# A fused attention and mixture-of-experts kernel: recurrent products in all four quadrants, counts by two blocks, eight tie blocks on GpSimd, other PSUM banks

## The chip, the cores and the metric

The kernel runs on one core of a Trainium2 chip. The metric is the device time of one execution in microseconds (us). The core has five engines with queues of their own: TensorE (PE in the profile, its weight loads PEld), VectorE (DVE), ScalarE (ACT), GpSimd (POOL) and SyncE (SP, which issues most DMAs). Each engine works its queue in order; semaphores tie them together.

## The reference

Three stages follow one another. The first is linear attention with a decaying state, over two batches, eight heads, 768 positions and head size 64:

```python
intra = (q_b @ k_b.T * Dmask) @ v_b                  # within a block
inter = (q_b * lam_pow) @ kv_state                   # from the blocks before
out[block] = intra + inter
kv_state = lam_block * kv_state + (k_b * rev_pow).T @ v_b
```

Its output, as 1536 tokens of 512 numbers, goes through a dense layer, `g = h * clip(h + 3, 0, 6) / 6` with `h = x @ w_in` (512 to 2048), then `x2 = g @ w_out` (2048 to 512). The third stage sends each token to one of eight experts: all pairs of token and expert are walked through from the highest logit down, a pair is taken if the token is still free and the expert has fewer than 192 tokens, and each token then goes through its expert, `relu(x2 @ w1[e]) @ w2[e]` (512 to 1024 to 512).

## The kernel before

Attention (`attention`, L425) works in twelve chunks of 128 positions, six a batch (`s = c % 6`). The head size is 64, so two heads of a pair share the 128 partitions; a chunk has four head pairs `hp` with two halves `par`. PE makes the scores `S` (L451), DVE masks them into `sm` (L457), PE multiplies the decayed keys `kd` with the values into `kv` (L466). The state lives in three SBUF tiles `sbd`: DVE fades the old one into the new (L471) and adds `kv` (L473); the first chunk of a batch only copies (L475). Then `outs` puts the chunk's output `xo` together in one PSUM bank, head pair by head pair: a product of the state with the decayed queries `qd` for each half (L489, if there is a state, which holds for ten of the twelve chunks) and one of `sm` with the values (L492). All are float32. Of a state product the operands of half 0 lie in partitions 0 to 63 and its output goes to 0 to 63, half 1 has 64 to 127 for both. ACT (L496) and DVE (L497) turn `xo` into two float16 halves of `xT`, which the dense layer takes.

Every product of the dense layer is three float16 products (`mm3`, L221 to L223, tile `h`). Its weights come as 64-bit integers, and `weights` decodes them on ACT, DVE (tiles `wid`, `wod`) and POOL. ACT and DVE make `g` from `h` (`r`, L526 and L527). The second layer is `x2_part` (L637, tile `x2p`): 48 matmuls for each of twelve token blocks, 512 columns wide for the first eight blocks, 384 for the last four, whose remaining 128 columns are made last (192 matmuls). Its output goes to `xa` and `xb`.

The routing runs beside x2: its logits come from `g` and a projected gate, and it takes seven phases. In each, PE spreads every token's current value over the partitions (`mp`, L738), ACT copies it to SBUF (`mrow`), and for each of twelve token blocks a mask `G` says which tokens come before which: below (L770) and at or below (L779) on DVE, four blocks on ACT for the first part. Tokens of equal value inside a block are ordered by a tie block `eq`: `BY_GE = 6` on POOL (L746, one selection over all at L748), the others on DVE (L753). PE counts with four matmuls a block (`count`, L792, tile `cp`) and twelve small ones for the ties (`ties`, L763). Then DVE compares with the capacity (`F`), PE spreads the result (`sm`, L809 and L810), and DVE settles the next phase. After the last phase come the ranks (`rk`) and positions (`pos`), POOL scatters the rows of `xa` and `xb` to DRAM (L840), they come back by expert (`xs`), and the experts run (`hp`, L885, `po`, L915).

The order of each engine's queue is written by a planner (`Plan`) when the kernel is built. It keeps a clock for each engine, and places the step that can begin first by its own costs, among those within a small window the one with the lowest key. A step with no free PSUM or SBUF slot in its pool waits. PSUM has eight banks in pools: pA 3, pB 2, pC 2, pE 1. Routing steps have the key `GK = -1e6` and go first; x2's matmuls fill PE's time between them, one at a time.

Of the kernel before, what the change touches and what calls it, by code (L numbers as in the profile page):

```python
# [5 lines left out]
F32 = mybir.dt.float32  # L6
# [9 lines left out]
P = 128  # L16
# [176 lines left out]
def fused_kernel(ctx, tc, raw_d, lam_d, win_d, wout_d, wg_d, w1_d, w2_d, out):  # L193
# [227 lines left out]
    out_done = {}  # L421
# [3 lines left out]
    def attention(c, key):  # L425
# [33 lines left out]
        if s < 5:  # L459
            pk = buf("pC", [P, 4, 64], F32, f"kv{c}")  # L460

            def kv():
                for hp in range(4):
                    for par in range(2):
                        cl = slice(P * hp + 64 * par, P * hp + 64 * par + 64)
                        te.matmul(pk[64 * par:64 * par + 64, hp], kd[:, cl], r[:, 2, cl], start=True, stop=True)  # L466
            t_kv = add("pe", 0.66, kv, [t_kd] + ld, [kd, r, pk], key)
# [26 lines left out]
        used = [r, po] + sms + ([qd, sbdb] if s else [])  # L494
        t_o = out_done[c] = add("pe", 3.9 if s else 1.95, outs, t_mk + t_qd + ld + (state_done[c - 1] if s else []), used, key)
        t_h = add("se", 0.48, lambda: se.activation(x[:, 0, :, t0:t0 + P], po[:], AF.Copy, scale=2.0 ** 10), [t_o], [po, x], key)  # L496
        x_done[c] = add("ve", c_ve(512), lambda: ve.scalar_tensor_tensor(  # L497
            x[:, 1, :, t0:t0 + P], po[:], 2.0 ** 10, x[:, 0, :, t0:t0 + P], op0=OP.mult, op1=OP.subtract), [t_h], [po, x], key)
# [6 lines left out]
    def h_unit(g, u, key, lo_eng):  # L505
# [17 lines left out]
        t = add("pe", 12 * nf * c_pe(T), mms, w_done[f0 % 4 // 2:(f0 % 4 + nf - 1) // 2 + 1] + [x_done[c] for c in cs], [w, x, ps], key)  # L523
# [42 lines left out]
    def project(k, t, dst):  # L566
# [11 lines left out]
        t_pj.append(add("pe", 0.5, pj, tr + [t_wg], [wt, wpp], key))  # L578
# [112 lines left out]
    BY_GE = 6  # L691
# [38 lines left out]
    for p in range(PHASES):  # L730
# [12 lines left out]
        eqs = [buf("Q", [P, 6, P], BF, f"eq{p}_{i}") for i in range(2)]  # L743
# [4 lines left out]
        t_eq = [add("ge", 1.3, lambda eq=eqs[0]: ge.affine_select(  # L748
# [10 lines left out]
        def ties(cp=cp, eqs=eqs):  # L759
            for f in range(3):  # L760
                for k in range(4):
                    b = 3 * k + f
                    te.matmul(cp[32 * k:32 * k + 32, P * f:P * f + P], ohc[:, b], eqs[b // BY_GE][:, b % BY_GE], start=False, stop=False)  # L763
        order_c = [0, 1, 2, 11, 3, 4, 10, 5, 9, 6, 8, 7]
        for n, i in enumerate(order_c):
# [24 lines left out]
            def count(i=i, n=n, G=G, z=z, cp=cp):  # L790
                for k in range(4):
                    te.matmul(cp[32 * k:32 * k + 32, :], ohc[:, i], G[:, z, 384 * k:384 * k + 384], start=(n == 0),  # L792
                              stop=(n == NCH - 1))
# [170 lines left out]
def pack(inputs):  # L964
# [12 lines left out]
    lam = np.repeat(np.asarray(inputs["lam"]).reshape(4, 2).T, 64, axis=0)  # L977
# [22 lines left out]
```

## Time and profile before

| | us |
|---|---|
| median of 3 runs | 525.7 (525.66 to 525.78) |
| the profiled execution | 526.52 |
| its span in the trace | 524.5 |
| PE busy | 498.5 (95%) |
| DVE busy | 404.6 (77%) |
| ACT busy | 300.6 (57%) |
| POOL busy | 156.0 (30%) |

The mean granted clock of PE is 0.983 of full speed. Busy shares are means over stages that differ: the dense layer with attention runs to about 205 us, the routing beside x2 to about 346, then come the ranks, the scatter and the rest of x2, and from 391 on the experts. A wait in a row of PE stands in brackets behind it, with the engine that ended it; "issue" means that nothing in the profile explains it.

### The profile page before, as it was taken

The page shows a single profiled execution, that of the slowest core. Times are in us where ns is not written, and L with a number is a line of the kernel's source. Part 1 is how long each engine was busy: PE and PEld are TensorE (multiplying, and loading weights), DVE is VectorE, ACT ScalarE, POOL GpSimd, SP SyncE. Part 2 cuts the span into 40 slices and gives each one's busy share as a digit, 9 for nine tenths or more (in the row PEclk, how much of TensorE's full clock was granted, in tenths as well). Part 3 has the DMA queues.
Part 4 walks back from the last instruction along what each step waited for, and adds up shares of the span by engine and source line. Part 5 has one row for each costly group of instructions (what it writes and reads, how often), then busy time and mean ns, then how long its engine had stood idle before and what let it go on. Part 6 is the DMA issues. An engine that isn't in the chain of part 4 may idle for free.

```text
span 524.5 us, 10556 instructions
## 1 busy us (share of the span) xinstructions
PE 498.5 (95%) x4378; PEld 304.5 (58%) x4378; DVE 404.6 (77%) x718; ACT 300.6 (57%) x444; POOL 156.0 (30%) x160
## 2 busy tenths in 40 slices
PE   7898999998999999999999999999499999999995
PEld 3566454687786444534433443466399577786762
DVE  7799999999534988699899888975242988889620
ACT  1547958563235574287669667843152867778610
POOL 2022424040000340055325523628811122223111
PEclk8999999999999999999999999999779999999999
DMA  7999524202537224000000001746454999998011
GB/s 217 396 417 413 196 87 164 81 2 53 142 129 161 41 41 81 2 1 1 1 2 1 1 0 56 267 176 212 118 144 125 358 332 417 290 377 349 4 41 40
DMA packets 44912, 77.88 MB, mean 148 GB/s; under 512 B 33081, under 2 KB 34113, under 8 KB 38721
## 3 DMA queue, kind: packets, MB, share of 16 engines
q1 hardware_dynamic: 42752, 70.82, 41.0%
q0 software_dynamic: 2112, 6.39, 3.3%
q8 instruction: 34, 0.56, 0.5%
q14 instruction: 14, 0.11, 0.1%
HBM read 63.46 MB, written 6.40 MB: 133 GB/s over the span
## 4 chain that ended last, share of the span: by engine, by line
PE 61%; DVE 21%; issue 9%; DMA 5%; ACT 2%; POOL 1%; POOLq 0%; SPq 0%; DVEq 0%; ACTq 0%
PE x2p L637 24%; PE hp L885 8%; PE po L915 6%; PE h L221 4%; PE h L222 4%; PE h L223 4%; PE cp L792 3%; DMA ws<-w 2%; DVE r L527 2%; DVE g L415 2%; DVE wid L388 2%; DVE wid L390 2%; PE mp L738 1%; DMA raw<-raw 1%; ACT kd L438 1%
## 5 line engine op out<-in xcount | busy, mean ns | idle before, releaser
L637 PE MATMUL x2p<-wo,g 128*128 128x512 f16 (+2 forms) x768 | 144.7, 334 | 7.5 <-issue 7.1
L637 PEld LDWEIGHTS <-g 128*128 128x128 f16 x768 | 65.4, 102 | 63.7 <-issue 22.5
L221 PE MATMUL h<-xT,wi 128*128 128x256 f16 (+2 forms) x304 | 88.3, 301 | 3.7 <-DVE r L527 3.7
L223 PE MATMUL h<-xT,wi 128*128 128x256 f16 (+2 forms) x304 | 88.2, 300 | 0.0
L222 PE MATMUL h<-xT,wi 128*128 128x256 f16 (+2 forms) x304 | 88.2, 300 | 0.0
L415 DVE SCALAR_TENSOR_TENSOR w<-ws,w 128x1024 f16<-128x1024 f32 x58 | 71.5, 1277 | 8.1 <-ACT w L405 7.3
L746 POOL TENSOR_SCALAR eq<-mrow,m 128x128 bf16<-128x128 f32 x42 | 47.3, 1142 | 85.4 <-DVE on L719 60.2
L405 ACT ACTIVATE w<-ws 128x1024 f16<-128x1024 f32 x64 | 64.3, 1049 | 2.9 <-DMA ws<-w 2.2
L885 PE MATMUL hp<-xs,w 128*128 128x192 f16 x768 | 65.1, 246 | 0.0
L885 PEld LDWEIGHTS <-w 128*128 128x128 f16 x768 | 63.1, 98 | 3.2 <-issue 1.6
L915 PE MATMUL po<-w,h 128*64 128x512 f16 (+1 forms) x384 | 64.1, 380 | 0.1
L384 POOL TENSOR_SCALAR wod<-wod 128x1024 f32<-128x1024 f32 x8 | 23.7, 2965 | 103.5 <-ACT wod L382 103.5
L526 ACT ACTIVATE r<-h,c 128x512 f32<-128x512 f32 (+1 forms) x52 | 33.3, 646 | 30.6 <-PE h L223 30.6
L779 DVE TENSOR_SCALAR G<-mrow,m 128x1408 bf16<-128x1408 f32 (+10 forms) x77 | 48.2, 648 | 0.0
L915 PEld LDWEIGHTS <-h 128*64 128x64 f16 (+1 forms) x384 | 29.0, 104 | 31.7 <-issue 1.6
L405 ACT ACTIVATE g<-r 128x512 f16<-128x512 f32 (+1 forms) x52 | 30.2, 592 | 23.0 <-DVE r L527 19.8
L415 DVE SCALAR_TENSOR_TENSOR g<-r,g 128x512 f16<-128x512 f32 (+1 forms) x52 | 35.7, 697 | 9.2 <-ACT g L405 8.8
L527 DVE SCALAR_TENSOR_TENSOR r<-r,h 128x512 f32<-128x512 f32 (+1 forms) x52 | 32.9, 640 | 11.4 <-ACT r L526 11.3
L222 PEld LDWEIGHTS <-wi 128*128 128x128 f16 x304 | 29.7, 98 | 17.3 <-issue 4.2
L773 ACT ACTIVATE G<-mrow,m 128x1536 bf16<-128x1536 f32 (+3 forms) x28 | 39.3, 1404 | 0.2
L221 PEld LDWEIGHTS <-wi 128*128 128x128 f16 x304 | 29.7, 98 | 14.8 <-issue 0.7
L223 PEld LDWEIGHTS <-wi 128*128 128x128 f16 x304 | 29.7, 98 | 14.6
(147 smaller groups left out, 685.1 us busy)
## 6 DMA issues: line engine op xcount, KB each, us to landing
ws<-w SPq DMA_DIRECT2D x32, 1024.0 KB, 9.3
raw<-raw SPq DMA_DIRECT2D x24, 512.0 KB, 9.8
wis<-w_in SPq DMA_DIRECT2D x8, 1024.0 KB, 14.9
wos<-w_out SPq DMA_DIRECT2D x8, 1024.0 KB, 6.3
tab<-tz SPq DMA_DIRECT2D x1, 512.0 KB
wt<-wo SPq DMA_TRANSPOSE x16, 3.4
xsa<-xa,pos POOLq DMA_INDIRECT x12
xsb<-xb,pos POOLq DMA_INDIRECT x12
```

The costliest lines, as they stand in the source:

```text
L221: te.matmul(ps, lh, rh, start=start, stop=False)
L222: te.matmul(ps, lh, rl, start=False, stop=False)
L223: te.matmul(ps, ll, rh, start=False, stop=stop)
L405: h = add("se", c_se(n), lambda: se.activation(dst()[0], src(), AF.Copy, scale=sc), deps, bufs, key, reserve)
L415: lo = add("ve", c_ve(n), lambda: ve.scalar_tensor_tensor(dst()[1], src(), sc, dst()[0], op0=OP.mult, op1=OP.subtract), [h], bufs, key)
L527: t = add("ve", c_ve(nf * T), lambda: ve.scalar_tensor_tensor(r[:], r[:], 6.0 * 2.0 ** -11, ps[:], op0=OP.min, op1=OP.mult), [t], [ps, r], ...
L637: te.matmul(ps[:], gsl(y, fc, j), w[:, z, fc % 4, d0:d1], start=(fc + y + z == 0), stop=(fc == 15 and y == 1))
L746: t_eq.append(add("ge", 1.06, lambda i=i, eq=eqs[0], mrow=mrow: ge.tensor_scalar(eq[:, i], mrow[:, P * i:P * i + P], m[:, i:i + 1], None, ...
L773: se.activation(G[:, z, 0:o], mrow[:, 0:o], AF.Sign, scale=-1.0, bias=m[:, i:i + 1])
L779: ve.tensor_scalar(G[:, z, o:], mrow[:, o:], m[:, i:i + 1], None, op0=OP.is_le)
L885: te.matmul(ps[:, i], w[:, z, kk % 2, cl], x[:, 2 * kk + y, CAP * i0:CAP * i0 + CAP], start=(i + kk + y + z == 0), stop=(i == 1 and kk == ...
L915: te.matmul(o, h1[e][:, y, k, cl], w2[e, fh][0][:, zz, f], start=(k + y + zz == 0), stop=(k == 7 and y == 1))
```

## The change

1. The host swaps the two partition halves of every odd head pair in q, k and lam. With that, a state product of an odd pair reads partitions 0 to 63 and writes 64 to 127, or the reverse. `outs` goes by halves `h2` of two head pairs: four state products, then four intra-chunk ones; even and odd pairs have a PSUM bank each (both of pC). ACT and DVE take `xT` from the two banks with two instructions each in place of one.
2. The fade of the state is done by ACT, in four instructions of 64 columns, and `kdec` is filled by four copies.
3. `kv` of the chunks from 4 on is in pool pE; the projection of the gate waits for `kv` of chunk 10.
4. `x2p` of each third token block is in pool pB.
5. A `count` step takes two blocks, and the ties come ahead of the last pair.
6. `BY_GE` is 8: POOL makes eight tie blocks and one selection over 1024 columns, DVE four, with a key ahead of the masks.

```diff
-            pk = buf("pC", [P, 4, 64], F32, f"kv{c}")
+            pk = buf("pE" if c > 3 else "pC", [P, 4, 64], F32, f"kv{c}")
...
-                        cl = slice(P * hp + 64 * par, P * hp + 64 * par + 64)
+                        cl = slice(P * hp + 64 * (par ^ hp & 1), P * hp + 64 * (par ^ hp & 1) + 64)
...
-                t = state_read[c] = add("ve", 0.35, lambda: ve.tensor_tensor(
-                    sb, old, pw[:, :, 256:257].to_broadcast([P, 4, 64]), op=OP.mult), war + state_done.get(c - 1, []), [tabb, sbdb], key)
+                def fade():
+                    for hp in range(4):
+                        se.activation(sb[:, hp], old[:, hp], AF.Copy, scale=pw[:, hp, 256:257])
+                t = state_read[c] = add("se", 0.8, fade, war + state_done.get(c - 1, []), [tabb, sbdb], key)
...
-        po = buf("pC", [P, 4, P], F32, f"xo{c}")
+        pos = [buf("pC", [P, 2, P], F32, f"xo{c}_{z}") for z in range(2)]
...
-            for hp in range(4):
-                for par in range(2):
-                    pr = slice(64 * par, 64 * par + 64)
-                    if s:
-                        te.matmul(po[pr, hp], sp[pr, hp], qd[pr, hp], start=True, stop=False)
-                for par in range(2):
-                    h = 2 * hp + par
-                    te.matmul(po[64 * par:64 * par + 64, hp], r[:, 2, 64 * h:64 * h + 64], sms[par][:, hp],
-                              start=(s == 0), stop=True)
+            for h2 in range(2):
+                if s:
+                    for z in range(2):
+                        for par in range(2):
+                            pr, o = slice(64 * par, 64 * par + 64), 64 * (par ^ z)
+                            te.matmul(pos[z][o:o + 64, h2], sp[pr, 2 * h2 + z], qd[pr, 2 * h2 + z], start=(h2 == 0), stop=False)
+                for z in range(2):
+                    for par in range(2):
+                        h = 2 * (2 * h2 + z) + par
+                        te.matmul(pos[z][64 * par:64 * par + 64, h2], r[:, 2, 64 * h:64 * h + 64], sms[par ^ z][:, 2 * h2 + z],
+                                  start=(s == 0 and h2 == 0), stop=(h2 == 1))
...
-        if j < JB:
-            x2_part(j, 0, 512, "pC", x_key + 11 * j)
-        else:
-            x2_part(j, 0, 384, "pC", x_key + 11 * j)
+        x2_part(j, 0, 512 if j < JB else 384, "pB" if j % 3 == 2 else "pC", x_key + 11 * j)
...
-    BY_GE = 6
+    BY_GE = 8
...
-                t_eq.append(add("ve", 0.27, lambda i=i, tie=tie: tie(i), [t_row[i // 4]], [eqs[1], mrow], GK + n))
+                t_eq.append(add("ve", 0.27, lambda i=i, tie=tie: tie(i), [t_row[i // 4], t_oh], [eqs[1], mrow], GK - 0.5))
...
+            group.append((i, z, G))
+            t_g += t
+            if len(group) < 2:
+                continue
```

The planner writes the queues anew from this. On PE, the first state chunk's output `xo` (chunk 1) began like this before; `qd` and `sbd` are the state product's operands, `sm_0` and `sm_1` the masked scores of the two halves:

```order
L489 MATMUL xo_317<-qd_238,sbd 64x128 x2
L492 MATMUL xo_317<-sm_0_248,raw_110 64x128
L492 MATMUL xo_317<-sm_1_278,raw_110 64x128
L489 MATMUL xo_317<-qd_238,sbd 64x128 x2
L492 MATMUL xo_317<-sm_0_248,raw_110 64x128
L492 MATMUL xo_317<-sm_1_278,raw_110 64x128
```

The same chunk on PE now (`xo_0` and `xo_1` are the two banks):

```order
L494 MATMUL xo_0_385<-qd_238,sbd 64x128 x2
L494 MATMUL xo_1_386<-qd_238,sbd 64x128 x2
L498 MATMUL xo_0_385<-sm_0_259,raw_110 64x128
L498 MATMUL xo_0_385<-sm_1_281,raw_110 64x128
L498 MATMUL xo_1_386<-sm_1_281,raw_110 64x128
L498 MATMUL xo_1_386<-sm_0_259,raw_110 64x128
```

Both pieces are half a chunk: four state products and four intra-chunk ones, in four turns before and in two now. On DVE, the second routing phase began like this before:

```order
L723 SCALAR_TENSOR_TENSOR ohc<-closed,oh 128x12x8
L770 TENSOR_SCALAR G_0_2842<-mrow_2827,m 128x128
L770 TENSOR_SCALAR G_0_2842<-mrow_2827,m 128x256
L779 TENSOR_SCALAR G_0_2842<-mrow_2827,m 128x1408
L779 TENSOR_SCALAR G_0_2842<-mrow_2827,m 128x1280
L770 TENSOR_SCALAR G_1_2866<-mrow_2827,m 128x384
L779 TENSOR_SCALAR G_1_2866<-mrow_2827,m 128x1152
L753 SCALAR_TENSOR_TENSOR eq_1_2878<-mrow_2827,m,before 128x128
L770 TENSOR_SCALAR G_1_2866<-mrow_2827,m 128x512
L779 TENSOR_SCALAR G_1_2866<-mrow_2827,m 128x1024
```

The same phase on DVE now:

```order
L729 SCALAR_TENSOR_TENSOR ohc<-closed,oh 128x12x8
L777 TENSOR_SCALAR G_0_2904<-mrow_2890,m 128x128
L777 TENSOR_SCALAR G_0_2904<-mrow_2890,m 128x256
L759 SCALAR_TENSOR_TENSOR eq_4_2911<-mrow_2890,m,before 128x128 x4
L786 TENSOR_SCALAR G_0_2904<-mrow_2890,m 128x1408
L786 TENSOR_SCALAR G_0_2904<-mrow_2890,m 128x1280
L777 TENSOR_SCALAR G_1_2936<-mrow_2890,m 128x384
L786 TENSOR_SCALAR G_1_2936<-mrow_2890,m 128x1152
L777 TENSOR_SCALAR G_1_2936<-mrow_2890,m 128x512
L786 TENSOR_SCALAR G_1_2936<-mrow_2890,m 128x1024
```

DVE's four tie blocks of a phase stand together ahead of the second half of the first masks; before, six were spread over the phase. On PE a phase from the second on held 10 matmuls of x2 before its first count and 57 in all, with nine interruptions by counts; now 19 stand before the first count and 38 before the ties, 58 in all, with six interruptions. The instructions after the ranks stand in the same order on every engine as before.

## Rows read from the trace of the kernel before

**Rows 1.** Stretches: start:end, length, busy PE, PEld, DVE, ACT, POOL, clock, DMA, GB/s

```profile
20.00:122.00 102.00, 95.62 (x960) 64.22 (x960) 99.77 (x141) 67.57 (x145) 28.20 (x9) 1.00 0.54 205
122.00:205.00 83.00, 81.59 (x694) 50.16 (x692) 60.55 (x84) 41.12 (x61) 11.41 (x4) 1.00 0.40 94
205.00:346.00 141.00, 140.71 (x1137) 62.46 (x1136) 124.06 (x320) 96.18 (x103) 55.63 (x52) 1.00 0.11 38
370.00:382.00 12.00, 4.89 (x35) 2.91 (x35) 2.44 (x3) 0.98 (x2) 8.27 (x14) 0.63 0.51 138
391.00:519.00 128.00, 127.44 (x1157) 92.17 (x1154) 86.47 (x112) 75.79 (x101) 29.39 (x32) 1.00 0.70 237
```

**Rows 2.** Waits of PE from 20 to 135 us: total, times, longest

```profile
PE h L221 <- DVE r L527: 3.7, 4, 1.3
```

**Rows 3.** Timeline of PE: start, length, line, tile, count [idle before <-releaser]; chunk 8

```profile
124.27 0.43 PE L489 MATMUL xo<-qd,sbd 64*64 64x128 f32 x4 [1.37 <-DVE sbd L473]
...
127.21 1.16 PE L451 MATMUL S<-raw 64*128 64x128 f32 x16
```

**Rows 4.** Timeline of PE: the first chunk, which has no state

```profile
16.22 1.09 PE L492 MATMUL xo<-sm,raw 128*64 128x128 f32 x16 [1.46 <-DMA raw<-raw]
17.12 1.46 PE L466 MATMUL kv<-raw,kd 128*64 128x64 f32 x16
```

**Rows 5.** Lines: duration ns min/median/max, first and last start us

```profile
L471 DVE TENSOR_TENSOR sbd<-sbd,tab x8: 415/424/861, 21.2 to 129.7; 128x256 f32<-128x256 f32 x8
L497 DVE SCALAR_TENSOR_TENSOR xT<-xo,xT x12: 682/684/692, 20.6 to 148.8; 128x512 f16<-128x512 f32 x12
L438 ACT ACTIVATE kd<-raw,kdec x80: 331/333/348, 16.2 to 98.9; 128x64 f32<-128x64 f32 x80
```

**Rows 6.** Timeline of PE in one phase of the routing (the second)

```profile
238.74 1.47 PE L738 MATMUL mp<-ident,m 128*128 128x128 f32 x12
240.05 2.32 PE L637 MATMUL x2p<-wo,g 128*128 128x512 f16 x10
242.30 0.35 PE L792 MATMUL cp<-G,ohc 128*32 128x384 bf16 x4
242.58 0.82 PE L637 MATMUL x2p<-wo,g 128*128 128x512 f16 x3
243.33 0.35 PE L792 MATMUL cp<-G,ohc 128*32 128x384 bf16 x4
...
244.58 0.51 PE L792 MATMUL cp<-G,ohc 128*32 128x384 bf16 x8
...
253.20 0.34 PE L763 MATMUL cp<-eq,ohc 128*32 128x128 bf16 x12
...
255.03 1.89 PE L637 MATMUL x2p<-wo,g 128*128 128x512 f16 x8
256.75 0.93 PE L738 MATMUL mp<-ident,m 128*128 128x128 f32 x7
```

**Rows 7.** Timeline of POOL in the same phase, and its tie line in all phases

```profile
240.07 6.78 POOL L746 TENSOR_SCALAR eq<-mrow,m 128x128 bf16<-128x128 f32 x6 [9.32 <-DVE on L719]
246.92 0.97 POOL L748 TENSOR_SCALAR_AFFINE_SELECT eq<-eq 128x768 bf16<-128x768 bf16 x1
...
L746 POOL TENSOR_SCALAR eq<-mrow,m x42: 622/1213/1812, 221.9 to 335.5; 128x128 bf16<-128x128 f32 x42
```

**Rows 8.** Timeline of DVE in the same phase: two masks of 512 columns

```profile
244.26 0.47 DVE L770 TENSOR_SCALAR G<-mrow,m 128x512 bf16<-128x512 f32 x1
...
251.85 0.47 DVE L779 TENSOR_SCALAR G<-mrow,m 128x512 bf16<-128x512 f32 x1
```

**Rows 9.** Timeline of PE from the end of x2 to the experts

```profile
370.43 0.22 PE L637 MATMUL x2p<-wo,g 128*128 128x128 f16 x1 [0.45 <-issue]
...
381.15 1.12 PE L637 MATMUL x2p<-wo,g 128*128 128x128 f16 x9 [0.43 <-issue]
...
391.11 2.06 PE L885 MATMUL hp<-xs,w 128*128 128x192 f16 x23
```

More of the change, by code (lines that the diff above doesn't have):

```diff
@@ L494, in attention @@
[L494 to L498, printed above, removed]
+            for h2 in range(2):
[4 more added lines that the diff above has]
+                            te.matmul(pos[z][o:o + 64, h2], sp[pr, 2 * h2 + z], qd[pr, 2 * h2 + z], start=(h2 == 0), stop=False)
+                for z in range(2):
+                    for par in range(2):
+                        h = 2 * (2 * h2 + z) + par
+                        te.matmul(pos[z][64 * par:64 * par + 64, h2], r[:, 2, 64 * h:64 * h + 64], sms[par ^ z][:, 2 * h2 + z],
+                                  start=(s == 0 and h2 == 0), stop=(h2 == 1))
@@ new lines, in attention @@
+        used = [r] + pos + sms + ([qd, sbdb] if s else [])
+        t_o = out_done[c] = add("pe", 3.0 if s else 1.6, outs, t_mk + t_qd + ld + (state_done[c - 1] if s else []), used, key)
+        done = []
+        for z in range(2):
+            t_h = add("se", 0.31, lambda z=z: se.activation(x[:, 0, z::2, t0:t0 + P], pos[z][:], AF.Copy, scale=2.0 ** 10), [t_o], [pos[z], x], key)
+            done.append(add("ve", 0.34, lambda z=z: ve.scalar_tensor_tensor(
+                x[:, 1, z::2, t0:t0 + P], pos[z][:], 2.0 ** 10, x[:, 0, z::2, t0:t0 + P], op0=OP.mult, op1=OP.subtract), [t_h], [pos[z], x], key))
@@ L501, in fused_kernel @@
+        x_done[c] = done
     gb, g_done = {}, {}
@@ L742, in fused_kernel @@
         t_oh = add("ve", 2.0 if p else 1.4, (lambda: (choose(), open_only())) if p else pick0, [t_m], [], GK)
-        eqs = [buf("Q", [P, 6, P], BF, f"eq{p}_{i}") for i in range(2)]
+        eqs = [buf("Q", [P, n, P], BF, f"eq{p}_{n}") for n in (BY_GE, NCH - BY_GE)]
         t_eq = []
@@ L762, in ties @@
                     b = 3 * k + f
-                    te.matmul(cp[32 * k:32 * k + 32, P * f:P * f + P], ohc[:, b], eqs[b // BY_GE][:, b % BY_GE], start=False, stop=False)
+                    te.matmul(cp[32 * k:32 * k + 32, P * f:P * f + P], ohc[:, b], eqs[b >= BY_GE][:, b % BY_GE], start=False, stop=False)
         order_c = [0, 1, 2, 11, 3, 4, 10, 5, 9, 6, 8, 7]
+        group, t_g = [], []
         for n, i in enumerate(order_c):
@@ L787, in fused_kernel, with count @@
             if i >= BY_GE:
-                t_eq.append(add("ve", 0.27, lambda i=i, tie=tie: tie(i), [t_row[i // 4]], [eqs[1], mrow], GK + n))
[L790 to L793, printed above, removed]
+                t_eq.append(add("ve", 0.27, lambda i=i, tie=tie: tie(i), [t_row[i // 4], t_oh], [eqs[1], mrow], GK - 0.5))
[3 more added lines that the diff above has]
+                continue
+            def count(group=group, n=n, cp=cp):
+                for i, z, G in group:
+                    for k in range(4):
+                        te.matmul(cp[32 * k:32 * k + 32, :], ohc[:, i], G[:, z, 384 * k:384 * k + 384], start=(n == 1 and i == group[0][0]),
+                                  stop=(n == NCH - 1 and i == group[1][0]))
             if n == NCH - 1:
-                t_c = add("pe", 0.4, ties, [t_c, *t_eq], eqs + [cp], GK)
-            t_c = add("pe", 0.24, count, t + [t_c, t_oh], [G, cp], GK)
+                t_c = add("pe", 0.2, ties, [t_c, *t_eq], eqs + [cp], GK)
+            t_c = add("pe", 0.44, count, t_g + [t_c, t_oh], [x[2] for x in group] + [cp], GK)
+            group, t_g = [], []
         t = t_c
@@ L976, in pack @@
     raw = np.stack([x.reshape(nb * c, P, 512) for x in parts], axis=2)
-    lam = np.repeat(np.asarray(inputs["lam"]).reshape(4, 2).T, 64, axis=0)
+    for x in (raw[:, :, 0], raw[:, :, 1]):
+        x = x.reshape(nb * c, 2, 64, 4, P)
+        x[:, :, :, 1::2] = x[:, ::-1, :, 1::2].copy()
+    lam = np.asarray(inputs["lam"]).reshape(4, 2).T.copy()
+    lam[:, 1::2] = lam[::-1, 1::2].copy()
+    lam = np.repeat(lam, 64, axis=0)
     wi = np.asarray(inputs["moe_w_in"]).reshape(4, P, 8, 256).transpose(2, 1, 0, 3)
```

14 lines of the change are left out of this document (7 added, 7 removed).

## The prediction

> **What bounds the kernel now.** On the page TensorE (PE) has by far the largest busy share, so a change gains about what it takes out of PE's queue, wherever PE is not waiting for something else. The table of stretches says where that is [rows 1]. From 20 to 122 us VectorE (DVE) is busy for 99.77 of 102 us and PE for 95.62: here DVE decodes weights and is the limit, and PE's waits say so (3.7 us in four waits of the first GEMM for DVE's product `r`, up to 1.3 us each) [rows 2]. From 122 to 205 us PE is busy for 81.59 of 83, from 205 to 346 (the routing) for 140.71 of 141, from 391 to 519 (the experts) for 127.44 of 128. In between lies one hole: from 370 to 382 us PE works for 4.89 of 12 us. There the last 128-column matmuls of x2 come in bursts, with waits that the profile calls "issue", until the row at 381.15; the experts start at 391.11 [rows 9]. The expert part has no slack, so whatever moves its start moves the end by as much.
>
> **The change, part by part.**
>
> *Recurrent products.* In the chunk at 124.27 PE goes from the first product to the next tile at 127.21 in 2.94 us [rows 3]: eight groups, by turns 64\*64 and 128\*64 in tiling, at 2.94/8 = 0.367 us. A chunk without state runs all its sixteen 128\*64 passes in one mode, two side by side, from 16.22 to 17.12: eight steps in 0.90 us, 0.11 each [rows 4]. In the new order a chunk has four groups: two 64\*64 groups that now use all four quadrants, and two 128\*64 groups with twice the passes. I price the first as before, 0.367, since four products side by side are as deep as two; the second is 0.367 + 2 x 0.11 = 0.587. A chunk takes 2 x (0.367 + 0.587) = 1.91 us and saves 1.03. Ten chunks have a state. No row of before shows four quadrants at once; if they run two after two, the 64\*64 group is 0.587 deep as well, the chunk takes 2.35 and saves 0.59.
>
> Five of these chunks lie where PE is at most waiting for itself (one at 96.5 us, four from 124.27 on): 5 x 1.03 = 5.2 us on the path. The other five lie in DVE's stretch, where PE's time is hidden behind DVE. There DVE decides: six of the eight state fades go (0.42 us each [rows 5]: -2.5 us), and eight evacuations of xT are cut in two. A whole one is 0.684 us for 512 columns; the fade's 0.424 for 256 gives 0.26 for 256 columns and so about 0.16 of fixed cost, which each cut adds once (+1.3 us). DVE has 1.2 us less to do, which I take as the gain of this stretch, 1.3 us; nothing of it is the lower bound, and the upper is 3.5, about PE's waits for DVE there [rows 2]. ScalarE's four small fades take 4 x 0.333 = 1.3 us at most (the copy of kd has their size [rows 5]), DVE's one took 0.42; the chain fade, sum, next chunk becomes up to 0.9 us longer. At 124.27 PE already waited 1.37 us for that chain [rows 3]. The new order puts the kv products earlier, in a bank of their own, which should take that wait away, and the longer chain may keep it: I count nothing, with 0 to 1.4 in the range. Sum for attention: 5.2 + 1.3 = **6.5 us**, between 4 (five chunks at 0.59, and 1 early) and 9 (5.2 + 3.5).
>
> *Counts by two blocks.* One phase of the routing takes 256.75 - 238.74 = 18.0 us, and there are seven [rows 6]. PE fills a phase with 57 matmuls of x2; eight of them take 1.72 us (255.03 to 256.75), 0.215 each. A single count costs 242.58 - 242.30 = 0.28 us, and a run of three x2 matmuls between two counts takes 243.33 - 242.58 = 0.75 us, 0.10 more than 3 x 0.215. A double count is 0.51 instead of 0.35 long, so 0.16 more than a single [rows 6]. Merging two singles saves 0.28 + 0.10 - 0.16 = 0.22 us. Nine interruptions become six: 0.66 us a phase. With 58 instead of 57 matmuls of x2 in the phase, it is 18.0 - 0.66 + 0.22, about 17.6 us: the ranks come 7 x 0.41 = 2.9 us earlier, and x2 as a whole is done 7 x 0.66 = 4.6 less about 0.2 = 4.4 us earlier.
>
> *Eight tie blocks on GpSimd.* GpSimd starts 1.33 us after the phase's first product, takes 6.78 us for six blocks and 0.97 for the selection: it ends at 247.89, 9.2 us into the phase, and PE uses the ties at 253.20, 14.5 us in [rows 6, 7]. Two blocks more at 1.13 and a selection of 0.97 x 8/6 = 1.29 (an estimate) end at 11.8 us. PE now reaches the ties after 38 matmuls of x2: 1.31 (from the first product to the first x2 matmul, 238.74 to 240.05) + 38 x 0.215 + 5 x 0.44 + 5 x 0.10 = 12.2 us in. The margin is 0.4 us, so GpSimd costs nothing, but the cover is nearly gone: each 0.1 us on every block puts 0.8 us on the phase once the margin is used. On DVE two tie blocks go (2 x 0.27) and four move ahead of the second half of the first pair of counts, which come 4 x 0.27 = 1.1 us later; 19 matmuls of x2 stand before the first count now, against 10, which is 1.9 us of cover. The later pairs on DVE are level with PE to some 0.3 us; I leave 0 to 0.4 us a phase (0 to 3 in all) as a loss, and take 0.
>
> By the Trainium skill, page "SBUF — State Buffer", section "Who interferes with whom", VectorE and GpSimd share a port as an exclusive lock, so that one waits wholly for the other. By that two more blocks of 0.62 us (GpSimd's shortest) could stop DVE for 1.24 us a phase where it gets back 0.54, some 5 us in seven phases. The rows speak against it for this form: DVE's 128x512 comparison takes 0.47 us at 244.26, with GpSimd at work, and 0.47 at 251.85, with GpSimd done [rows 8]; it is GpSimd whose blocks spread from 0.622 to 1.812 [rows 7].
>
> *x2 in a third bank, kv in its own.* A third bank frees PE from DVE's evacuation; PE hardly waits for it in the routing (0.3 of 141 us), so it is worth nothing, to +0.3. The projections now wait for the tenth chunk's kv product; the products they sat behind come first anyway: nothing.
>
> *The hole at 370 us.* The order after the ranks is the same on every engine. The bursts end about when the gathered rows of the experts arrive, and GpSimd's scatters run through them (8.27 of 12 us [rows 1]). If the hole hangs on the scatters, it moves with the ranks and the experts start 6.5 + 2.9 = 9.4 us earlier; if it has a fixed length, with x2, 6.5 + 4.4 = 10.9. From the side of the unpriced losses (0 to 3 us in DVE's pairs, half of it) 1 us comes off. I take **9 us**.
>
> The profiled execution took 526.52 us, 2.0 more than its span of 524.5 and 0.8 more than the median of 525.7. 526.52 - 9 = 517.5 in its own terms, which is 525.7 - 9 = **516.7 us** as a median.
>
> **The rivals.**
>
> *Quadrants in pairs.* If four products don't run side by side, ten chunks save 0.59: five late ones give 3.0, and the rest as above, 1.3 + 2.9 - 1 = 6.2 to 7 us in all: 519. For it: no row of before has more than two. Against it: two on the diagonal do run together.
>
> *DVE takes it.* The early stretch gives nothing and PE meets new waits for DVE's pairs in the routing at the upper bound: 5.2 + 2.9 - 3, about 4 to 5 us: 521.5. For it: 99.77 of 102 us; against it: DVE's own list gets shorter in both places.
>
> *The hole shrinks.* No wait in the profile explains it. If the shift of 1.5 us between ranks and x2 takes the tail out of it, up to 10 us go on top: 507. Against it: the same order on all engines.
>
> *Slower: GpSimd late.* PE waits for eight blocks in each phase. With a mean block of e, GpSimd ends at 1.33 + 8e + 1.29, against 12.2: no wait to e = 1.2, and 8 x (e - 1.2) us a phase above it. Nine us over seven phases are 1.28 a phase, so from e = 1.36 on the kernel is slower than before; at 1.45 it is 14 us, some 530. For it: the median of 1.213 and single blocks up to 1.812 [rows 7], which six in a row averaged out to 1.13; against it: those six took the same 6.7 to 6.8 us in each phase.
>
> **How the numbers follow.** The forecast (all four parts as priced) 0.6, quadrants in pairs 0.12, DVE takes it 0.12, the hole shrinks 0.08, GpSimd late 0.08 (of which 0.05 ends slower and 0.03 within a few us of before). Range: the forecast's own bounds are 4 + 2.9 - 1 = 6 and 9 + 4.4 = 13.4 us of gain, 512 to 520; taking in the DVE case it reaches to 522.5, and the quadrant case lies within: 511.5 to 522.5 leaves out the hole, GpSimd and little else. A difference under about 0.2% (1 us) can't be told from none in this kernel's runs. Faster by more 0.9, within 0.05, slower 0.05.
>
> **What would show it.** Right: a chunk's products of about 1.9 us with four quadrant rows at one start; phases of about 17.6 us; GpSimd's selection ending before the tie products; the ranks some 9 us and the experts' first row some 9 to 11 us earlier (near 382). Wrong: chunks of 2.3 us; PE waits named after `eq` or `G` in the routing; a hole of another length than 11 us ahead of the experts.

## The result, and the profile of the changed kernel

The changed kernel took 519.88 us (median of 4 runs, 518.49 to 520.86) against 525.74 us before (4 runs, 525.66 to 526.39): 0.9884 of the time, 95% interval 0.9859 to 0.9909. That is 5.9 us less, where 9 were forecast (516.7 us); it lies inside the range and on the forecast side. The profiled execution is the quickest of the four, 518.49 us with a span of 516.7, so its span is 7.8 us shorter than before. Run again on two other chips (e8 and e12, below), the changed kernel took 8.9 and 7.6 us less than the kernel before.

The page's first part for the changed kernel, busy time by engine, and two of its groups (instructions of a line, busy us, mean ns of one):

```profile
PE 485.8 (94%) x4381; PEld 301.6 (58%) x4383; DVE 398.9 (77%) x710; ACT 309.3 (60%) x488; POOL 163.5 (32%) x174
...
L752 POOL TENSOR_SCALAR eq<-mrow,m 128x128 bf16<-128x128 f32 x56 | 56.7, 1030 | 84.5 <-DVE on L725 52.1
...
L786 DVE TENSOR_SCALAR G<-mrow,m 128x1408 bf16<-128x1408 f32 (+10 forms) x77 | 52.0, 706 | 0.0
```

The stretches of the changed kernel (columns as in [rows 1]; the fourth is its hole, which now lies from 361 to 373 us):

```profile
20.00:122.00 102.00, 95.99 (x1036) 67.65 (x1034) 97.45 (x146) 74.21 (x181) 24.36 (x8) 0.98 0.53 202
122.00:205.00 83.00, 82.16 (x762) 49.91 (x763) 64.08 (x96) 45.19 (x72) 13.83 (x5) 1.00 0.39 96
205.00:346.00 141.00, 138.51 (x1079) 64.31 (x1069) 122.93 (x307) 96.07 (x101) 69.70 (x69) 1.00 0.13 47
361.00:373.00 12.00, 3.50 (x18) 1.41 (x18) 2.97 (x3) 2.38 (x3) 7.80 (x16) 0.61 0.47 120
384.00:512.00 128.00, 126.64 (x1146) 91.36 (x1143) 85.40 (x111) 75.33 (x100) 29.50 (x33) 1.00 0.69 237
```

From 20 to 122 us DVE is no longer full (97.45 of 102 us). From 205 on PE is idle for 2.5 us where it was idle for 0.3 before. The waits of PE in that stretch name the cause (total us, times, longest); before there was no wait for `G` in this list:

```profile
PE cp L805 <- DVE G L786: 2.5, 7, 0.5
```

A chunk's output in the changed kernel, the timeline of PE at chunk 8 (beside [rows 3]). Eight state products stand in one row of 0.45 us where four stood in one of 0.43, and two such turns make the chunk:

```profile
117.76 0.45 PE L494 MATMUL xo<-qd,sbd 64*64 64x128 f32 x8
118.14 0.66 PE L498 MATMUL xo<-sm,raw 128*64 128x128 f32 x8
118.73 0.45 PE L494 MATMUL xo<-qd,sbd 64*64 64x128 f32 x8
119.11 0.66 PE L498 MATMUL xo<-sm,raw 128*64 128x128 f32 x8
```

From 117.76 to the second turn at 118.73 are 0.97 us, so a chunk takes 1.94 us (priced at 1.91), and the wait of 1.37 us ahead of chunk 8 is gone.

The second phase of the routing in the changed kernel: PE's rows around the fourth pair of counts, DVE's masks at that time, and GpSimd's row (beside [rows 6] and [rows 7]):

```profile
239.16 1.04 PE L646 MATMUL x2p<-wo,g 128*128 128x512 f16 x4
240.13 0.50 PE L805 MATMUL cp<-G,ohc 128*32 128x384 bf16 x6
240.93 0.34 PE L805 MATMUL cp<-G,ohc 128*32 128x384 bf16 x2 [0.30 <-DVE G L786]
241.20 1.04 PE L646 MATMUL x2p<-wo,g 128*128 128x512 f16 x4
```

```profile
238.87 0.65 DVE L777 TENSOR_SCALAR G<-mrow,m 128x768 bf16<-128x768 f32 x1
239.44 1.70 DVE L786 TENSOR_SCALAR G<-mrow,m 128x768 bf16<-128x768 f32 x2
```

```profile
239.18 1.28 POOL L754 TENSOR_SCALAR_AFFINE_SELECT eq<-eq 128x1024 bf16<-128x1024 bf16 x1
```

The pair of counts takes 241.20 - 240.13 = 1.07 us in place of 0.44 (as at 235.26 to 235.70 in this phase). It waits for a mask of 768 columns, which begins at 239.44, 0.26 us after GpSimd's selection. That mask takes 1.43 us, and 1.70 with the small one behind it; the mask of the same 768 columns just ahead took 0.65. The bracket shows only 0.30 us of the delay, because the six rows ahead of the wait count as busy until 240.63. GpSimd's selection ends at 240.46, ahead of the ties, as forecast.

Set side by side, the spans of the two profiled executions differ like this (starts of the first rows of each tile):

| stretch | before | changed | difference | forecast |
|---|---|---|---|---|
| start to the first chunk's output | 16.2 | 14.8 | -1.4 | none |
| from there to the first routing phase | 204.4 | 196.3 | -8.1 | -6.5 |
| first phase to the ranks | 127.8 | 129.9 | +2.2 | -2.9 (up to 3 less) |
| ranks to the experts | 42.8 | 42.3 | -0.5 | none |
| experts to the end | 133.4 | 133.4 | 0 | none |

### The profile page after: what moved, and what is told of

Same layout as the page of the kernel before. It is cut to its first block, busy times and chain, and to the rows that moved or that the text cites. A ratio compares the mean times of both kernels' runs of the same rounds, so it can differ in the third digit from the quotient of the medians.

```text
span 516.7 us, 10599 instructions
## 1 busy us (share of the span) xinstructions
PE 485.8 (94%) x4381; PEld 301.6 (58%) x4383; DVE 398.9 (77%) x710; ACT 309.3 (60%) x488; POOL 163.5 (32%) x174
## 4 chain that ended last, share of the span: by engine, by line
PE 47%; DVE 30%; issue 10%; ACT 5%; DMA 5%; POOL 1%; POOLq 0%; DVEq 0%; ACTq 0%; SPq 0%
PE x2p L646 14%; PE hp L899 9%; DVE G L786 7%; PE po L929 6%; PE h L221 5%; PE h L222 4%; PE h L223 4%; DVE G L777 3%; DMA ws<-w 3%; ACT kd L439 2%; DVE sm L458 2%; DVE g L416 2%; DVE eq L759 2%; PE cp L805 2%; DVE r L536 2%
## 5 line engine op out<-in xcount | busy, mean ns | idle before, releaser
L646 PE MATMUL x2p<-wo,g 128*128 128x512 f16 (+2 forms) x768 | 140.0, 332 | 9.0 <-issue 9.0
L221 PE MATMUL h<-xT,wi 128*128 128x256 f16 (+2 forms) x304 | 89.5, 303 | 1.8 <-DVE r L536 1.8
L222 PE MATMUL h<-xT,wi 128*128 128x256 f16 (+2 forms) x304 | 89.4, 303 | 0.0
L223 PE MATMUL h<-xT,wi 128*128 128x256 f16 (+2 forms) x304 | 89.3, 303 | 0.0
L752 POOL TENSOR_SCALAR eq<-mrow,m 128x128 bf16<-128x128 f32 x56 | 56.7, 1030 | 84.5 <-DVE on L725 52.1
L786 DVE TENSOR_SCALAR G<-mrow,m 128x1408 bf16<-128x1408 f32 (+10 forms) x77 | 52.0, 706 | 0.0
L385 POOL TENSOR_SCALAR wod<-wod 128x1024 f32<-128x1024 f32 x8 | 22.5, 2819 | 89.3 <-ACT wod L383 75.5
L416 DVE SCALAR_TENSOR_TENSOR g<-r,g 128x512 f16<-128x512 f32 (+1 forms) x52 | 34.4, 665 | 11.3 <-ACT g L406 10.8
L221 PEld LDWEIGHTS <-wi 128*128 128x128 f16 x304 | 30.1, 99 | 15.1 <-issue 1.6
L222 PEld LDWEIGHTS <-wi 128*128 128x128 f16 x304 | 30.1, 99 | 14.8 <-issue 2.1
L223 PEld LDWEIGHTS <-wi 128*128 128x128 f16 x304 | 30.1, 99 | 14.7
## 6 DMA issues: line engine op xcount, KB each, us to landing
wis<-w_in SPq DMA_DIRECT2D x8, 1024.0 KB, 14.8
```

The source lines that it names most:

```text
L221: te.matmul(ps, lh, rh, start=start, stop=False)
L222: te.matmul(ps, lh, rl, start=False, stop=False)
L223: te.matmul(ps, ll, rh, start=False, stop=stop)
L416: lo = add("ve", c_ve(n), lambda: ve.scalar_tensor_tensor(dst()[1], src(), sc, dst()[0], op0=OP.mult, op1=OP.subtract), [h], bufs, key)
L646: te.matmul(ps[:], gsl(y, fc, j), w[:, z, fc % 4, d0:d1], start=(fc + y + z == 0), stop=(fc == 15 and y == 1))
L752: t_eq.append(add("ge", 1.06, lambda i=i, eq=eqs[0], mrow=mrow: ge.tensor_scalar(eq[:, i], mrow[:, P * i:P * i + P], m[:, i:i + 1], None, ...
```

## Experiments

The runs stand in three groups, each on a chip of its own with its own runs of the kernel before: e1 to e4, e5 to e8 and e9 to e12. On the first of these chips the kernel before took 525.74 us, as in the result; on the other two 519.4. The table of stretches further down shows where that difference lies.

**e1, e2: each half alone.** e1 takes the hunks of attention, e2 those of the routing and of x2's banks; in e1 the routing lines stand as before:

```diff
-    BY_GE = 8
+    BY_GE = 6
...
-                t_eq.append(add("ve", 0.27, lambda i=i, tie=tie: tie(i), [t_row[i // 4], t_oh], [eqs[1], mrow], GK - 0.5))
+                t_eq.append(add("ve", 0.27, lambda i=i, tie=tie: tie(i), [t_row[i // 4]], [eqs[1], mrow], GK + n))
...
-            group.append((i, z, G))
-            t_g += t
-            if len(group) < 2:
-                continue
```

> The attention half of the change alone (state products in four quadrants, xT from two banks, fade on ScalarE, kv in pE); routing, counts, ties and x2's banks as before. Theory A (the attention half brought more than priced, the routing half took some of it back): the first routing phase starts near 211 us, phases take 18.0 us, the ranks come near 339 us, some 2 us ahead of the changed kernel's 341.0, and the time is 517 to 518.5 us. Theory B (each half pays about as forecast, 6.5 and 2.9 us less the losses): phases of 18.0, ranks near 342, 520 to 521 us.

> The routing half alone (counts by two, eight tie blocks on GpSimd, four tie blocks early on VectorE, a third of x2 in pB); attention as before. Theory A: phases of 18.2 us, with TensorE waiting 0.3 us for a mask in each; ranks 0 to 1.5 us later than before (348.4 to 350), time 525 to 527 us. Theory B: phases of 17.6 to 17.8, ranks 2 to 3 us earlier, time 522 to 523.5 us.

e1 took 516.85 us, 0.9827 of before (0.9806 to 0.9848): the attention half alone is 8.9 us faster. e2 took 526.96 us, 1.0025 (1.0012 to 1.0038): the routing half alone is 1.2 us slower. From the first phase to the ranks, e1 takes 128.2 us and e2 130.2, against 127.8 before. e2's list of PE's waits from 205 to 350 us has the changed kernel's row, with attention as before:

```profile
PE cp L796 <- DVE G L777: 2.0, 6, 0.4
```

In the times and in the stretch up to the ranks theory A holds: the routing half costs what it was to bring. Its places don't all fit: e2's ranks come at 350.7 us, 2.3 later than before where at most 1.5 were expected, and e1's at 342.9 in place of 339. The profiled execution of e1 is the slowest of its five (520.63 us, the others 516.18 to 517.61), so its stretches show the routing well and the whole gain badly. The halves don't add up exactly (-8.9 + 1.2 = -7.7 against -5.9 for both). The profiled e1 needed 40.5 us from the ranks to the experts against 42.3, with a hole of only 3.4 us and a wait of 3.2 us for DVE behind it; whether the other runs of e1 did the same is not shown.

**e3: a short selection.** The selection covers one tie block, and GpSimd compares with a constant, so that its blocks hold no ties:

```diff
-                eq[:, i], mrow[:, P * i:P * i + P], m[:, i:i + 1], None, op0=OP.is_equal), [t_row[i // 4]], [eqs[0], mrow], GK))
+                eq[:, i], mrow[:, P * i:P * i + P], c3, None, op0=OP.is_equal), [t_row[i // 4]], [eqs[0], mrow], GK))
...
-            out=eq[:], in_=eq[:], pattern=[[0, BY_GE], [1, P]], compare_op=OP.is_gt, fill=0.0, base=0,
+            out=eq[:, 0:1], in_=eq[:, 0:1], pattern=[[0, 1], [1, P]], compare_op=OP.is_gt, fill=0.0, base=0,
```

> The changed kernel with GpSimd's selection over one tie block in place of eight (128 columns, about 0.2 to 0.4 us in place of 1.28); so that nothing is counted wrongly, GpSimd's eight blocks compare with a constant and hold no ties: ties inside those blocks are left out. The order on all engines is the changed kernel's. Theory A (the long selection holds up VectorE's 128x768 mask, and TensorE waits for that mask): the mask takes 0.55 to 0.6 us, TensorE's wait for masks (2.5 us in seven) is gone, phases of 17.6 us, ranks about 4 us earlier (337), time some 3 to 4 us under the changed kernel's. Theory C (the masks are late because four tie blocks now go ahead of them): the mask may be shorter, but waits of 0.2 us or more and phases of 18.0 to 18.2 stay.

515.52 us, 0.9812 (0.9789 to 0.9836), 4.4 us under the changed kernel's 519.88. The order of PE is the changed kernel's to the row, so the phase can be read beside it. In e3's second phase, DVE's two masks of 768 columns, GpSimd's selection and PE's fourth pair read:

```profile
240.01 0.61 DVE L777 TENSOR_SCALAR G<-mrow,m 128x768 bf16<-128x768 f32 x1
240.54 0.93 DVE L786 TENSOR_SCALAR G<-mrow,m 128x768 bf16<-128x768 f32 x2
```

```profile
241.28 0.33 POOL L754 TENSOR_SCALAR_AFFINE_SELECT eq<-eq 128x128 bf16<-128x128 bf16 x1
```

```profile
241.50 0.51 PE L805 MATMUL cp<-G,ohc 128*32 128x384 bf16 x8
241.94 1.04 PE L646 MATMUL x2p<-wo,g 128*128 128x512 f16 x4
```

The two masks take 0.93 in place of 1.70 us, the pair of counts 0.44 in place of 1.07, and no wait of PE for a mask is left in the routing. Most phases are 17.57 us; from the first phase to the ranks are 125.1 us, 4.8 less than in the changed kernel and 2.7 less than before. The four early tie blocks are still there, so theory C falls.

**e4: tie blocks spread again.**

```diff
-                t_eq.append(add("ve", 0.27, lambda i=i, tie=tie: tie(i), [t_row[i // 4], t_oh], [eqs[1], mrow], GK - 0.5))
+                t_eq.append(add("ve", 0.27, lambda i=i, tie=tie: tie(i), [t_row[i // 4]], [eqs[1], mrow], GK + n))
```

> The changed kernel with VectorE's four tie blocks back among the masks (key as before). Theory C: the fourth pair of counts no longer waits, phases of 17.6 to 17.8 us, ranks 3 to 4 us earlier. Theory A: the mask that meets the selection still takes over 1.1 us; as each mask stands up to 1.1 us earlier, TensorE's wait may shrink, but phases stay over 17.9 us.

518.67 us, 0.987 (0.9849 to 0.9891); phases of 18.0 to 18.2 us. The selection (240.02, 1.59 us) now met the masks of the fifth pair (128x640 and the one behind it: 1.70 us in place of 0.87), and the fifth pair of counts took 0.81 us in place of 0.44; the planner also set the ties apart from the fifth pair, one interruption more. The delay moved with the selection, as theory A has it; the phase as a whole holds that interruption too.

**e5: tie blocks under the selection.** The same line, with the key `GK + 7.5`:

```diff
-                t_eq.append(add("ve", 0.27, lambda i=i, tie=tie: tie(i), [t_row[i // 4], t_oh], [eqs[1], mrow], GK - 0.5))
+                t_eq.append(add("ve", 0.27, lambda i=i, tie=tie: tie(i), [t_row[i // 4]], [eqs[1], mrow], GK + 7.5))
```

> The changed kernel with VectorE's four tie blocks placed behind the fourth pair of masks, where GpSimd's long selection runs. Theory A1 (the selection stops VectorE's masks but not its tie blocks, which read two tensors): the four tie blocks take their 1.1 to 1.3 us while the selection runs, no mask takes over 1.1 us, TensorE's waits for masks go, phases of 17.6 to 17.8 us, ranks some 3 us earlier than in the changed kernel, time about 516.5 to 517.5 us. Theory A2 (the selection stops any instruction of VectorE): the tie blocks take up to 2 us in a row, the pair behind them is late, phases stay at 18.0 to 18.3 and the time within 1 us of the changed kernel's.

511.34 us, against 510.55 of the changed kernel on the same chip (e8), so no gain; phases of 18.0 to 18.2 us. A1 falls. DVE's row with the four tie blocks and GpSimd's selection, in e5's second phase:

```profile
240.06 2.12 DVE L759 SCALAR_TENSOR_TENSOR eq<-mrow,m,before 128x128 bf16<-128x128 f32 x4
```

```profile
240.95 1.09 POOL L754 TENSOR_SCALAR_AFFINE_SELECT eq<-eq 128x1024 bf16<-128x1024 bf16 x1
```

Four tie blocks take 2.12 us here and 1.17 in e3, where none meets the selection. So the selection stops the tie blocks too, not only the masks. The masks behind them are late for the fifth pair of counts, which takes 0.76 us in place of 0.44, as A2 has it.

**e6: six tie blocks on GpSimd.**

```diff
-    BY_GE = 8
+    BY_GE = 6
```

> The changed kernel with six tie blocks on GpSimd in place of eight (selection over 768 columns, 0.97 us as before), six on VectorE ahead of the masks; counts by two as changed. Theory A: a mask that meets the selection is still held up, by some 0.3 us less; but VectorE has two tie blocks more (0.54 us) ahead of its masks, so the masks are later: phases of 18.2 to 18.5 us, time 519 to 521. If the eight blocks as such were the cost (GpSimd's length, not the meeting), phases would fall to 17.6 to 17.8.

512.68 us, 2.1 more than the changed kernel on that chip; phases of 18.5 to 18.6 us. With six tie blocks ahead of the masks, DVE is late for the second pair already, and the selection (238.14, 0.87 us) meets the mask of 1152 columns, which takes 1.42 us in place of 0.83. GpSimd's length as such is not the cost. GpSimd's six blocks took 4.96 us here and 6.78 before [rows 7]. The first four stood beside DVE's tie blocks at 0.63 to 0.66 us each, the last two beside masks at 1.25 and 1.21:

```profile
233.10 2.54 POOL L752 TENSOR_SCALAR eq<-mrow,m 128x128 bf16<-128x128 f32 x4 [10.76 <-DVE on L725]
235.62 2.45 POOL L752 TENSOR_SCALAR eq<-mrow,m 128x128 bf16<-128x128 f32 x2
```

**e7: x2 in one width.**

```diff
-    JB = 8
+    JB = 12
```

> The changed kernel with x2's last four token blocks 512 columns wide like the first eight, so that no 128-column matmuls stand behind them. On the hole of 12 us ahead of the experts. Theory H1 (all engines are slow to issue while GpSimd scatters the narrow rows, whatever TensorE has in its queue): TensorE still stands in bursts, a hole of 8 to 13 us in which it waits for nothing the profile shows. Theory H2 (only the short matmuls and their weight loads fall behind): no hole, x2 ends about 365 us, the experts start when the gathered rows are there, some 5 to 10 us earlier, time 510 to 515 us.

522.6 us, against 510.55 (e8): 12 us slower, where 510 to 515 us were expected without a hole. The question stays open, since e8 has no hole on this chip either. What e7 shows is the wait behind it: the experts stood for the gathered rows, by PE's waits from 345 us on:

```profile
PE hp L899 <- DMA xs<-xsa: 13.8, 1, 13.8
```

The edit brought this wait itself. The gather needs all twelve of GpSimd's scatters of `xsa`. In e8 the last of them stands at 366.79, behind four scatters of `xsb`; in e7 the planner put eleven of `xsb` ahead of it, and it stands at 376.39:

```profile
376.39 0.96 POOL L854 DMA_INDIRECT xsa<-xa,pos  x1 [0.19 <-DVE w L416]
```

**e8, e9, e11, e12: the same kernels again.** No edit in e8, e12 (the changed kernel) and e9 (the kernel before); e11 is e1.

> The changed kernel as it is, beside the others. Theory S (the early part varies from run to run with the arrival of the decay table by DMA, and everything behind moves with it): the first chunk's products start between 14.5 and 17 us, the seventh chunk's between 93 and 96.5 us, behind that the stretches have the same lengths as before to 0.3 us; times of 518 to 521 us. Otherwise the spread arises in the hole ahead of the experts, and the seventh chunk starts at 93.0 us again.

> The kernel before as it is, for its stretches on the chip of these runs. Theory S: the first phase starts near 220.5 us, phases of 18.0 us, ranks near 348.3; the time from the ranks to the experts is 42 to 43 us where TensorE has the hole and near 32 us where it has none, and the whole time follows it (526 or 516 us).

> The attention half alone once more, on the chip of the other runs. Theory A: from the first phase to the ranks 128 us, 2 us less than the changed kernel; time 1 to 3 us under the changed kernel's if the stretch from the ranks to the experts is the same in both.

> The changed kernel once more, on the chip of the other runs. Theory S: from the first phase to the ranks 130 us; from the ranks to the experts 32 us without a hole, 42 us with one; the seventh chunk's products between 93 and 96.5 us.

e8 took 510.55 us (0.982, 0.9766 to 0.9874), e12 511.78 (0.9818, 0.9772 to 0.9864), e11 513.66 (0.9893, 0.9842 to 0.9945), e9 520.56 in its one run. The stretches of the profiled executions:

| | 1st chunk to 7th's output | 7th chunk's output at | 1st phase to ranks | ranks to experts | experts to the end |
|---|---|---|---|---|---|
| before (result) | 80.3 | 96.5 | 127.8 | 42.8 | 133.4 |
| e9, before | 80.3 | 97.0 | 127.8 | 33.6 | 136.2 |
| changed (result) | 78.1 | 93.0 | 129.9 | 42.3 | 133.4 |
| e8, changed | 79.1 | 95.2 | 130.0 | 31.8 | 133.3 |
| e12, changed | 78.4 | 95.2 | 129.7 | 32.5 | 135.9 |
| e1, attention half | 80.5 | 96.4 | 128.2 | 40.5 | 135.4 |
| e11, attention half | 78.1 | 95.0 | 128.3 | 34.9 | 135.4 |

(The chunk that is called the seventh here is the one at 96.5 us in the kernel before.) The routing repeats to 0.3 us on all chips. The time from the ranks to the experts has two sizes: 40 to 43 us in the traces of the result and of e1 to e4, 31 to 35 in those of e5, e6 and e8 to e12 (e7's 42.2 us are its late scatter). There the hole is absent, and PE waits for the gathered rows instead, in e11 for DVE. In e12 PE's rows from 350 us to the experts are two:

```profile
349.72 22.26 PE L646 MATMUL x2p<-wo,g 128*128 128x384 f16 x262
375.62 2.72 PE L899 MATMUL hp<-xs,w 128*128 128x192 f16 x16 [3.64 <-DMA xs<-xsa]
```

So e8's expectation, that only the early part varies (518 to 521 us), missed. As it was put again for e9 and e12, theory S is right about the hole as a thing of its own, which came with both kernels in the traces of the first chips and with neither on the last. In the early part the new order gives starts of the seventh chunk between 93.0 and 96.4 us where the old one gives 96.5 to 97.0. e11 is 1.9 us slower than e12 where 1 to 3 us faster was expected, although its ranks come 1.6 us earlier: it has more of x2 left behind the ranks, in two banks, and waits 3.5 us for DVE there, and its experts start right behind x2. So the routing half's cost is shown up to the ranks; on this chip the kernel with it is the faster one by the medians.

e9 was expected at 516 us without a hole and took 520.56, because the experts took longer, 136.2 us: it gains 9.2 us ahead of them and loses 2.8 in them. Just before, PE had stood for the gathered rows, 3.5 us in e9 and 2.9 in e8. The first 3.7 us of the experts in e9 and in e8 (columns as in [rows 1]):

```profile
382.30:386.00 3.70, 3.70 (x24) 3.40 (x24) 0.00 (x0) 0.70 (x1) 2.13 (x4) 0.50 1.07 335
375.30:379.00 3.70, 3.68 (x45) 3.67 (x45) 0.00 (x0) 0.00 (x0) 2.55 (x6) 1.00 1.07 280
```

In e9 the granted clock was 0.50, the lower level of 1.2 GHz, for 24 matmuls in place of 45, then 0.72 from 386 to 390 us and 1.00 behind; in e8 it stayed at 1.00. The length of the wait alone doesn't tell which: e6 waited 3.7 us, kept 1.00, and needed 133.3 us for the experts.

**e10: the selection on VectorE.** GpSimd keeps the comparisons; DVE makes the selection as one product behind its last mask, and the tie products go behind the last pair of counts:

```diff
-        t_eq = [add("ge", 1.7, lambda eq=eqs[0]: ge.affine_select(
-            out=eq[:], in_=eq[:], pattern=[[0, BY_GE], [1, P]], compare_op=OP.is_gt, fill=0.0, base=0,
-            channel_multiplier=-1), t_eq, [eqs[0]], GK)]
+        t_ge, t_eq = t_eq, []
...
             if n == NCH - 1:
+                t_eq.append(add("ve", 1.0, lambda eq=eqs[0]: ve.tensor_tensor(
+                    eq[:], eq[:], before.unsqueeze(1).to_broadcast([P, BY_GE, P]), op=OP.mult), t_ge, [eqs[0]], GK + n))
                 t_c = add("pe", 0.2, ties, [t_c, *t_eq], eqs + [cp], GK)
```

> The changed kernel with the selection over GpSimd's eight tie blocks taken from GpSimd and done by VectorE behind its last mask, as one product with the triangle (128x1024, 16-bit); the tie products stand behind the last pair of counts. Theory A: no mask is held up, waits of TensorE for masks under 0.3 us in all, phases of 17.5 to 17.7 us, from the first phase to the ranks some 125 to 126 us in place of 130, time 3.5 to 4.5 us under the changed kernel's on the same chip. If instead GpSimd's comparisons hold VectorE up too, or VectorE's product (0.6 to 1.1 us) makes the ties late, phases stay at 18 us or more.

507.33 us, 0.9766 of before (0.9721 to 0.9812), 4.45 us under the changed kernel on the same chip (e12, 511.78). DVE's product and PE's last pair with the ties in e10's second phase:

```profile
242.75 0.68 DVE L807 TENSOR_TENSOR eq<-eq,before 128x1024 bf16<-128x1024 bf16 x1
```

```profile
243.88 0.51 PE L803 MATMUL cp<-G,ohc 128*32 128x384 bf16 x8
244.22 0.34 PE L767 MATMUL cp<-eq,ohc 128*32 128x128 bf16 x12
```

The product ends at 243.43, 0.8 us ahead of the ties. PE waits for no mask, the phase takes 247.61 - 230.04 = 17.57 us, and from the first phase to the ranks are 125.2 us. It leaves nothing out and beats both kernels.

## Why the prediction was right or wrong

**The recurrent products: right, and the sum in part by luck.** Four quadrants run at once (eight rows in 0.38 us where four took 0.37), a chunk takes 1.94 us against 1.91 priced, so the rival of quadrants in pairs is out. From the first chunk's output to the first phase the changed kernel needs 8.1 us less; 1.1 of it are five x2 matmuls that now come later (33 in place of 38 ahead of the first phase, 0.215 each), and 7.0 us stand against the forecast 6.5. Within it, the early stretch to the seventh chunk gave 2.2 us in the profiled run (1.3 taken, 3.5 as the bound) but 1.2 to 2.6 in the other runs of the changed order (2.2 in e11), and nothing in the profiled e1. The wait of 1.37 us ahead of chunk 8 went, for which I had counted nothing; between the seventh and the eighth chunk 2.9 us went in every run. From chunk 8 to chunk 11 2.4 us went, not 3 x 1.03, and in chunk 11 PE now waits 0.8 us for a mask of scores. So the stretch from the seventh chunk on gave 4.8 us of the 5.2 priced for five chunks, and 1.4 of these 4.8 are the wait that I had counted at nothing: the products alone brought less on the path than they save in a chunk.

**Counts by two: right in size, and lost elsewhere.** The forecast phase was 17.6 us. With the long selection off GpSimd the phase is 17.57 us (e3, e10), and the ranks come 2.6 to 2.7 us earlier behind the first phase than before, where 2.9 were forecast. (The prediction's own 0.66 - 0.22 is 0.44 us a phase, not 0.41, which makes 3.1.)

**The step that failed** is the sentence on DVE's later pairs, "level with PE to some 0.3 us", with a loss of "0 to 0.4 us a phase", of which I took none (and 1 us in the sum for all unpriced losses). It was 0.63 us a phase, 4.8 us to the ranks with the first phase (129.9 against 125.1), more than the 3 us that the rival on DVE gave it at most. The margin was read rightly: PE's last two rows of the pair would have followed the six before them at some 240.3 us, and a mask of 0.64 us, as without the selection in e3, would have ended at 240.08. Held up by 0.8 us, it ended at 240.88, and PE went on at 240.93. But I looked for GpSimd's effect on DVE at the wrong two rows. The masks of [rows 8] stand beside GpSimd's comparisons and beside nothing. The mask that met the selection was not among them, though the trace of before had it, in DVE's timeline of the same phase:

```profile
247.09 1.22 DVE L770 TENSOR_SCALAR G<-mrow,m 128x768 bf16<-128x768 f32 x1
```

It begins within the selection's 0.97 us from 246.92 on [rows 7], and a mask of 768 columns elsewhere takes 0.60 to 0.65. The same stands in each of the seven phases of before: one mask of 768 columns at 1.21 to 1.22 us, the other at 0.60 to 0.61. Before, PE came to that mask's count later, and nobody waited. The change made the selection longer (1.28 us), put it on a mask that PE needs at once, and moved four tie blocks ahead of the masks, which left DVE some 0.2 us of reserve.

By the Trainium skill, page "SBUF — State Buffer", section "Who interferes with whom", VectorE and GpSimd share a port as an exclusive lock. The prediction set the rule aside and priced it at 5 us. For the selection the runs agree with it (0.93 against 1.70 us for two masks, 1.17 against 2.12 for four tie blocks). That the loss of 4.8 us lies close to the price is chance: the price was for two more comparisons, not for the selection. The same section says that an instruction of VectorE with two inputs in SBUF meets GpSimd's reads too; the tie blocks of e5 agree. GpSimd's comparisons gave way instead: they take 1.21 to 1.25 us beside masks and 0.63 to 0.66 beside tie blocks (e6), and DVE's masks keep their length to about 0.1 us. Which of the two begins first bears on it: in e4 DVE's mask of 896 columns began at 239.99, just ahead of the selection at 240.02, and kept its 0.67 us, while the selection took 1.59 us in place of the 1.09 of e5. Whether the length of the selection or its kind matters besides, no run separates.

**GpSimd late: did not come.** GpSimd's eight comparisons took 8.0 us a phase (1.0 each, 1.13 were taken) and the selection 1.28, as estimated, and they ended 2.0 us ahead of the ties. GpSimd was the cause of the loss by what it held up, not by being late.

**The hole: right in the main.** Its end moved with the ranks (32.1 us behind them, 32.8 before), and the time from the ranks to the experts stayed within 0.5 us. Its length did not stay: 12.5 us, from 360.6, where the last row at pace ends, to 373.13, against 11.2 before. With PE's waits for `G`, that is the second of the prediction's signs of being wrong that came. That it comes and goes with the chip or its state could not be seen from one trace; e8, e9 and e12 show both kernels without it.

**The sum.** In the profiled run -1.4 - 8.1 + 2.2 - 0.5 = -7.8 us. The total is right in part by luck: the routing was to bring 2.9 us and cost 2.2, and an earlier start of 1.4 us, which no part of the change accounts for (14.8 us here, 16.1 and 16.8 in e8 and e12, 16.2 before), made up for some of it. The median gained only 5.9. The profiled run is 1.1 to 2.4 us quicker than the other three, which have no trace. The early part of the new order varies by 3.4 us from run to run in the traces and the experts' stretch by 2.6 us (133.3 to 135.9 in its own traces), and either would do; which of them is the cause of the spread here is not shown.

## What to carry to other kernels

When work is moved to GpSimd, look at each of its instructions apart, and at VectorE's rows at the very time that it runs: short comparisons gave way here, while one long selection stopped the masks and tie blocks that VectorE had next. A reserve that hides such a stop is spent when the same change moves other work ahead of it, so price the stop against what will be waited for after the change. And a stretch without a named wait, such as the hole here, is to be looked at on a second chip before anything is built on its length.

## What the runs showed of the hardware

One GpSimd selection over 128x1024 16-bit elements takes 1.09 to 1.59 us, and VectorE's instructions that met it were 0.8 to 1 us longer in all (e4, e5 and the changed kernel; 0.6 us beside 128x768, in e6 and before); VectorE does the same selection as a product in 0.68 us. The hole ahead of the experts, in which PE issues one to four matmuls at a time (3.5 of 12 us busy, granted clock 0.61), came in the traces of two of the four sets of runs, with either kernel; the time from the ranks to the experts is 9 to 10 us longer with it (42.8 against 33.6 us before, 42.3 against 31.8 and 32.5 in the changed kernel); an `xa` row of ACT begins in it at 363.57, 4.8 us after PE's last 384-column matmul for it had begun, so it is not PE alone that stands. Its cause stays open: it waits for no semaphore that the profile shows, and no run here tells what starts or ends it. The last 16 KB transfer of the queue of instructions ahead of it takes 0.97 us (at 357.32 in the changed kernel), 0.98 in e8 without a hole (at 359.64). Without it, PE's granted clock fell to 0.50 in e9 after a wait of 3.5 us for the gathered rows and stayed at 1.00 in e6 after one of 3.7.
